# Six weight blocks converted inside the feed-forward part, and first quarters loaded and split earlier

## The chip, the cores and the metric

The kernel runs on one core of one Trainium2 chip. The metric is the device time of one execution in microseconds, lower is better. Engines are named as in the profile: PE is TensorE (PEld its weight loads), DVE is VectorE, ACT is ScalarE, POOL is GpSimd, SP is SyncE, which here only issues DMAs.

## The reference

A long convolution filters the product `x * v` along the sequence (12480 tokens, 128 channels), and two feed-forward layers with 2048 hidden units each follow:

```python
u = x * v
y = irfft(rfft(u, n=2 * S) * rfft(h_filt, n=2 * S))[:S]
x = x * y
h = x @ moe_w_in;   g = h * clip(h + 3, 0, 6) / 6;                  x = g @ moe_w_out
h = x @ moe2_w_in;  g = where(h > 0, h, exp(minimum(h, 0)) - 1);    out = g @ moe2_w_out
```

The four weight matrices arrive as float64 words (as int64) and have to become pairs of single-precision numbers, an upper and a lower part.

## The kernel before

**Two parts.** Lines up to 794 compute the convolution as four steps of dense Fourier products. The fourth step (`fourth`, products of L677 into `y`, in the order of `PARTS`) closes 17 groups; after each, `leave_y` multiplies `y` into `xp` on DVE (L754, L757). From line 795 the feed-forward part runs: 25 tiles of up to 512 tokens, for each tile 8 units of layer 1 (m = 1) and 8 of layer 2 (m = 2, 13 units behind). A unit is six products into `h` (`mm1`, L878; `h<-xs` in layer 1, `h<-x` in layer 2), an activation on ACT (`act1`, L888 for layer 1, L890 for layer 2, with a clip on POOL, L891), a gate on DVE (`gate`, L899 and L901), the upper part of the result on ACT (`hi`, L907), the lower part on DVE (`lo`, L912) and six products into `o` (`mm2`, L922). A product of 128x128 by 128x512 is issued every 0.227 us, so that 12 of them, one unit's worth, take 2.72 us.

**What sets the order.** The program is a manual schedule: each engine runs its instructions in the order in which the code wrote them, and waits where an instruction needs another engine's result. In the feed-forward loop, step n runs the list `stages`: a unit's products at step n, its `mm2` 4 (layer 1) or 5 (layer 2) steps later. `h` has three buffers, so a unit's `mm1` waits for the gate of an earlier unit; `mm2` waits for `lo`.

**Weight conversion.** `JOBS` lists 32 blocks of 256 columns (4 matrices times 8). `weight_steps` converts one block per step: a load from `in_mw` (256 KB, on SP, L262), two ACT operations (L277, L278), three DVE operations (L289, L291, L292; called a *word* below), an addition on POOL (L295) and a store of 128 KB to `w_scratch` in DRAM (L272). `convert` spreads the steps over the convolution; ten of them fall into the fourth step (`steps`).

**Weight quarters.** The feed-forward part holds each matrix in four quarters `W[i, q]` of 512 columns. `load_w` brings one back from `w_scratch` (256 KB, L737), `rounded` makes the upper part on ACT (L740), and POOL subtracts for the lower part, in one piece (`split_w`, L745) or two halves (`lower_halves`, L825). The first three, `early`, have memory of their own. The others take over the memory of the convolution's buffers; the first four of them are requested ahead of the loop. The table `pieces` gives, for each quarter, the steps n of its two halves; its upper part is made a step earlier, its load asked for five steps earlier. `lower_halves` makes POOL wait for the last gate or `lo` written before it ("pace").

**Inputs.** `split` (L838, L840) turns a tile of `xp` into its upper part (ACT) and lower part (DVE); tile 1's runs ahead of the loop.

Of the kernel before, what the change touches and what calls it, by code (L numbers as in the profile page):

```python
# [135 lines left out]
def tile_kernel(ctx, tc, xc, vc, xT, posT, w1_d, w2_d, moe_w, t1_d, gm_d, cs_d, ti_d, rows_d, column_d, ratio_d, outT):  # L136
# [17 lines left out]
    def cut(buf, size, n):  # L154
        return [buf[:, i * size:(i + 1) * size] for i in range(n)]
# [143 lines left out]
            yield  # L299
        store(len(jobs) - 1)  # L300

    weights = weight_steps(JOBS, cut(cv, 2 * WC, 3), cut(cv[:, 6 * WC:], WC, 2), cut(cv[:, 8 * WC:], WC, 4))
    RATE = 0.75
    due = [0.0]

# [309 lines left out]
    def table(i):  # L615
        return lambda: load_ti(i)
# [102 lines left out]
    def new_y(i):  # L719
# [8 lines left out]
    x0 = xs[0]  # L728

    pieces = {  # L730
        (1, 0): (1, 1), (0, 3): (1, 2), (1, 1): (3, 4), (1, 2): (5, 6), (1, 3): (7, 8), (2, 0): (9, 10), (2, 1): (11, 12),
        (3, 0): (13, 15), (2, 2): (17, 18), (3, 1): (19, 20), (2, 3): (21, 22), (3, 2): (23, 24), (3, 3): (26, 28),
    }
    next_w = list(pieces)[:4]

# [3 lines left out]
    def rounded(w):  # L739
        nc.scalar.copy(w[:, 0], w[:, 1].bitcast(F32))  # L740

    def split_w(i, q, engine=nc.gpsimd):
        w = W[i, q]
        rounded(w)
        engine.tensor_tensor(  # L745
            out=w[:, 1], in0=w[:, 1].bitcast(F32), in1=w[:, 0].bitcast(F32), op=ALU.subtract
        )

    def leave_y(i, y, widths):
        o = START.get((BATCHES[i][0][0], 1), 0)  # L750
        if len(set(widths)) == 1:
            n, w = len(widths), widths[0]
            z = xp[:, o:o + n * w].rearrange("p (b n) -> p b n", n=w)
            nc.vector.tensor_tensor(out=z, in0=y[:, :n, :w], in1=z, op=ALU.mult)  # L754
        else:
            for b, w in enumerate(widths):
                nc.vector.tensor_tensor(out=xp[:, o:o + w], in0=y[:, b, :w], in1=xp[:, o:o + w], op=ALU.mult)  # L757
                o += w
        if i == 2:
            nc.scalar.copy(x0[:, 0], xp[:, :TT])  # L760
        if i in (12, 14, 15):
            split_w(*early[(12, 14, 15).index(i)])
# [8 lines left out]
    xc6, xc7 = map(part, xs_c[6:])  # L771
    weight = [lambda p=p: load_w(*p) for p in early]
    bunches = {
        ("r", 1): [xc6, table(7)], ("m", 1): [table(8), table(9)], ("r", 6): [table(10), table(11), table(12), xc7],
        ("m", 6): [table(13)], ("r", 9): [table(14), table(15)], ("m", 10): [table(16), weight[0]], ("r", 13): weight[1:],
        ("m", 14): [],
    }
    steps = (1, 2, 4, 6, 7, 8, 10, 11, 12, 13)
    begun = {}
    for kind, i in [(kind, i) for kind, a, b in PARTS for i in range(a, b)]:  # L780
        done = i in begun
# [19 lines left out]
    for k, ((i, q), ns) in enumerate(pieces.items()):  # L801
        W[i, q] = wp.tile([128, 2, WQ], F32R, name=f"w{i}_{q}")
        if k < 4:
            load_w(i, q)
        if k > 1:
            rounds.setdefault(ns[0] - 1, []).append((i, q))
        if k > 0:
            for h, n in enumerate(ns):
                halves.setdefault(n, []).append((i, q, h))
        if k > 3:  # L810
            loads.setdefault(ns[0] - 5, []).append((i, q))

    split_w(*next_w[0])
    rounded(W[next_w[1]])

    def round_at(n):
        for p in rounds.get(n, []):
            rounded(W[p])
        for p in loads.get(n, []):
            behind(load_w(*p), paced[0])  # L820

    def lower_halves(n):
        for i, q, h in halves.get(n, []):
            w = W[i, q][:, :, h * WQ // 2:(h + 1) * WQ // 2]
            lower = nc.gpsimd.tensor_tensor(  # L825
                out=w[:, 1], in0=w[:, 1].bitcast(F32), in1=w[:, 0].bitcast(F32), op=ALU.subtract
            )
            tc.add_manual_dep(
                lower.ins, last_dve[0].ins.name,
                mybir.DependencyInfo(mybir.DependencyClass.Sync, mybir.DependencyReason.DATA), reason="pace",  # L830
            )
# [99 lines left out]
                later.setdefault(k, []).append(lambda: leave(k, m, t))  # L931


    split(-1, 1, 1, xp[:, TILES[1]])
    later.pop(0)[0]()
    stages = (
        (act1, 2, 1), (mm1, 1, 0), (lo, 2, 4), (act1, 1, 0), (gate, 1, 0), (mm2, 1, LAG - 1), (hi, 2, 3),
        (hi, 1, 1), (gate, 2, 2), (mm1, 2, 0), (lo, 1, 1), (mm2, 2, LAG),
    )
    xin[1, 0] = x0  # L940
    assert not set(halves) - set(range(1, 14)) - set(range(15, len(units)))
    for n in range(len(units) + LAG + 2):
        for f in later.pop(n, []):
            done = f()
            if done:
                last_dve[0] = done[0]
        if NU < n < len(units) and units[n][0] == 1 and units[n][2] == 2:
            load_x(n, units[n][1] + 1)
        for f, m, delay in stages:
            if 0 <= n - delay < len(units) and units[n - delay][0] == m:  # L950
                if f is gate:
                    lower_halves(n)
                f(n - delay)
            if n == 1 and f is act1 and m == 1:
                round_at(n)
        if n != 1:
            round_at(n)


# [46 lines left out]
```

## Time and profile before

| | |
|---|---|
| median of 3 runs | 1319.63 us (1319.28 to 1320.71) |
| profiled execution | 1321.85 us, its span 1320.1 us |
| PE busy | 1310.8 us of the span (99%) |
| DVE, ACT, POOL busy | 1133.2, 1006.2, 412.0 us |
| mean granted clock | 0.999 of 2.4 GHz |

The profiled execution is 2.2 us above the median, and lies 1.75 us around its span. The fourth step runs from about 215 to 252 us of the span, the feed-forward part from 251.63 us to the end. Busy shares are means over stages; which engine waits for which is read stage by stage.

### The profile page before, as it was taken

Reading aid. Unit: us, or ns where it says so; the run is one execution under the profiler, and the core shown is the slowest. Engines: PE = TensorE matmul, PEld = TensorE weight load, DVE = VectorE, ACT = ScalarE, POOL = GpSimd, SP = SyncE. Lnnn points to the kernel's source line nnn. Section 1 sums busy time; section 2 is a strip of 40 time slices with the busy share of each in tenths; the row PEclk is TensorE's granted clock in tenths of the full one; section 3 lists DMA queues with packets and bytes.
Section 4 is the critical chain, followed back from the end, with each engine's and each line's share of the span. In section 5 each row is a group of like instructions: output and inputs, shape, how many; then the busy total and the mean of one; then the engine's idle time right before and its main releaser. Section 6 shows DMA issues by size and latency. Waiting matters only on the chain.

```text
span 1320.1 us, 23000 instructions
## 1 busy us (share of the span) xinstructions
PE 1310.8 (99%) x9184; PEld 1126.8 (85%) x9184; DVE 1133.2 (86%) x1210; ACT 1006.2 (76%) x1210; POOL 412.0 (31%) x317
## 2 busy tenths in 40 slices
PE   9999999999999999999999999999999999999998
PEld 8999999888888888888888888888888888888898
DVE  6769976889988888888888888888888888898897
ACT  5677663598877888788878887888788878887876
POOL 1027741334222232323232222222222223322223
PEclk9999999999999999999999999999999999999999
DMA  8834447610000000000000000000000000000000
GB/s 276 262 124 148 133 138 234 186 48 17 9 9 0 9 8 8 9 1 9 9 9 0 9 9 8 0 9 8 8 1 9 8 9 1 8 8 9 8 3 18
DMA packets 33676, 58.80 MB, mean 45 GB/s; under 512 B 3962, under 2 KB 10272, under 8 KB 33568
## 3 DMA queue, kind: packets, MB, share of 16 engines
q1 hardware_dynamic: 28816, 53.07, 13.1%
q10 hardware_dynamic: 4752, 4.26, 0.9%
q8 instruction: 72, 1.18, 0.4%
q14 instruction: 36, 0.29, 0.1%
HBM read 46.73 MB, written 10.58 MB: 43 GB/s over the span
## 4 chain that ended last, share of the span: by engine, by line
PE 93%; DMA 2%; DVE 1%; issue 1%; ACT 1%; POOL 1%; SPq 0%; ACTq 0%; POOLq 0%; DVEq 0%
PE o L922 40%; PE h L878 39%; PE pa L401 4%; PE q L501 2%; PE z L473 2%; PE y L677 2%; PE r L454 1%; PE h L463 1%; PE q L539 1%; DMA uv<-in_vc 1%; DMA qb<-in_posT 1%; DMA w<-w_scratch 0%; POOL a L891 0%; DVE qb L487 0%; DVE au L487 0%
## 5 line engine op out<-in xcount | busy, mean ns | idle before, releaser
L922 PE MATMUL o<-gs,w 128*128 128x512 f32 (+1 forms) x2400 | 565.5, 384 | 0.0
L922 PEld LDWEIGHTS o<-gs,w 128*128 128x128 f32 x2400 | 445.2, 188 | 85.1
L891 POOL TENSOR_SCALAR a<-a 128x1024 f32<-128x1024 f32 (+1 forms) x200 | 296.6, 1483 | 707.1 <-ACT a L890 706.8
L912 DVE TENSOR_TENSOR gs<-g,gs 128x1024 fp32r<-128x1024 f32 (+1 forms) x400 | 481.1, 1203 | 5.2 <-ACT gs L907 4.4
L907 ACT CAST gs<-g 128x1024 fp32r<-128x1024 f32 (+1 forms) x400 | 409.9, 1025 | 53.1 <-DVE g L899 51.6
L899 DVE SCALAR_TENSOR_TENSOR g<-a,h 128x1024 f32<-128x1024 f32 (+1 forms) x200 | 238.7, 1194 | 116.5 <-ACT a L888 116.3
L878 PE MATMUL h<-xs,w 128*128 128x512 f32 (+1 forms) x1200 | 298.0, 384 | 1.1 <-DVE g L899 1.1
L878 PE MATMUL h<-x,w 128*128 128x512 f32 (+1 forms) x1200 | 298.0, 384 | 0.2 <-ACT a L890 0.2
L890 ACT ACTIVATE a<-h 128x1024 f32<-128x1024 f32 (+1 forms) x200 | 201.5, 1007 | 89.4 <-PE h L878 87.8
L878 PEld LDWEIGHTS h<-xs,w 128*128 128x128 f32 x1200 | 223.2, 188 | 45.8 <-DVE g L899 1.7
L878 PEld LDWEIGHTS h<-x,w 128*128 128x128 f32 x1200 | 223.1, 188 | 43.8 <-issue 0.5
L888 ACT ACTIVATE a<-h,bounds 128x1024 f32<-128x1024 f32 (+1 forms) x200 | 218.9, 1095 | 49.1 <-PE h L878 48.6
L901 DVE SCALAR_TENSOR_TENSOR g<-a,h 128x1024 f32<-128x1024 f32 (+1 forms) x200 | 237.4, 1187 | 0.2 <-POOL a L891 0.2
L295 POOL TENSOR_TENSOR cv<-cv 128x256 int32<-128x256 int32 x32 | 23.4, 732 | 121.0 <-DVE cv L292 114.7
L401 PE MATMUL pa<-tab,qb 98*64 98x180 f32 x512 | 42.7, 316 | 0.0
L401 PEld LDWEIGHTS pa<-tab,qb 98*64 98x64 f32 x512 | 39.0, 138 | 2.1
L825 POOL TENSOR_TENSOR w<-w 128x256 fp32r<-128x256 f32 x24 | 17.8, 742 | 36.3 <-DVE gs L912 17.3
L277 ACT ACTIVATE cv<-cv 128x256 int32<-128x256 uint32 x32 | 14.3, 447 | 18.7 <-DMA cv<-in_mw 10.6
L677 PE MATMUL y<-ub,qb 52*64 52x97 f32 (+3 forms) x832 | 28.2, 247 | 0.1
L677 PEld LDWEIGHTS y<-ub,qb 52*64 52x64 f32 (+1 forms) x832 | 27.0, 137 | 1.1 <-DVE au L754 0.3
L854 ACT COPY y<-o 128x512 f32<-128x512 f32 (+1 forms) x25 | 14.5, 578 | 16.7 <-PE o L922 16.7
L492 POOL TENSOR_TENSOR au<-qb,au 128x1024 f32<-128x1024 f32 (+1 forms) x12 | 26.9, 2244 | 0.5 <-DVE au L487 0.5
(101 smaller groups left out, 874.4 us busy)
## 6 DMA issues: line engine op xcount, KB each, us to landing
cv<-in_mw SPq DMA_DIRECT2D x32, 256.0 KB
uv<-in_xc SPq DMA_DIRECT2D x32, 196.0 KB
out_T<-y SPq DMA_DIRECT2D x23, 256.0 KB
qb<-in_gm SPq DMA_DIRECT2D x22, 256.0 KB
au<-in_xT SPq DMA_DIRECT2D x16, 268.0 KB
w_scratch<-cv ACTq DMA_DIRECT2D x32, 128.0 KB
w<-w_scratch SPq DMA_DIRECT2D x16, 256.0 KB
cv<-in_vc SPq DMA_DIRECT2D x20, 196.0 KB
```

The costliest lines, as they stand in the source:

```text
L401: nc.tensor.matmul(pa[f * HN:(f + 1) * HN, j, :2 * NK], lhsT=src(j, f), rhs=table[:, f], start=True, stop=True)
L492: nc.gpsimd.tensor_tensor(out=spectrum(hf, k0 + a, n), in0=m1, in1=m2[:, :, :, ::-1], op=ALU.add)
L677: anchor[0] = nc.tensor.matmul(y[c * HD:(c + 1) * HD, b, off:off + w], lhsT=lhsT, rhs=rhs[:, H1 - w:], start=(b, c) in fresh, stop=done, s ...
L878: nc.tensor.matmul(h[:, j], lhsT=wslice(2 * m - 2, a, 2 * u + j), rhs=x[:, b], start=i == 0, stop=i == 2)
L888: paced[0] = nc.scalar.activation(a, h, AF.Relu, bias=three)
L890: nc.scalar.activation(a, h, AF.Exp)
L891: nc.gpsimd.tensor_scalar(a, a, 1.0, 0.0, op0=ALU.min, op1=ALU.max)
L899: last_dve[0] = nc.vector.scalar_tensor_tensor(g, a, 6.0, h, op0=ALU.min, op1=ALU.mult)
L901: last_dve[0] = nc.vector.scalar_tensor_tensor(g, a, -1.0, h, op0=ALU.add, op1=ALU.max)
L907: nc.scalar.copy(t[:, 0], g)
L912: last_dve[0] = nc.vector.tensor_tensor(out=t[:, 1], in0=g, in1=t[:, 0].bitcast(F32), op=ALU.subtract)
L922: nc.tensor.matmul(o[:, :WID[t]], lhsT=wslice(2 * m - 1, a, 2 * u + j), rhs=gs[:, b, j], start=u == 0 and i == 0, stop=u == NU - 1 and i + ...
```

## The change

- `weight_steps` gets the first 26 blocks (`FRONT`); the fourth step holds four conversion steps (after groups 2, 6, 9, 11) and no longer ten.
- The last six blocks, quarters 1 to 3 of matrix 3, are converted in the feed-forward loop, at steps 6, 10, 15, 21, 25 and 29 (`tail`, `block_parts`). For block n: two ACT operations at the end of step n-2 (`low`), the word on DVE at the end of step n-1, POOL's addition at the start of step n's gate (`total`), the upper part on ACT at the end of step n, the lower part on POOL a step later. They use one raw buffer and two sums, and go to the weight tile without the way over DRAM. Three quarters thus lose their load, their upper part of 512 columns and their two POOL halves.
- The early quarters are requested after groups r1, m6 and m10 and split after groups 5, 9 and 13 (before: m10 and r13; 12, 14, 15).
- Ahead of the loop, three quarters are split in one piece, with no pace (before: one split, one rounded). The table `pieces` gets other steps for the rest.
- The split of tile 1's input moves from ahead of the loop to step 4.

```diff
+    FRONT = 26
+    weights = weight_steps(JOBS[:FRONT], cut(cv, 2 * WC, 3), cut(cv[:, 6 * WC:], WC, 2), cut(cv[:, 8 * WC:], WC, 4))
...
     pieces = {
-        (1, 0): (1, 1), (0, 3): (1, 2), (1, 1): (3, 4), (1, 2): (5, 6), (1, 3): (7, 8), (2, 0): (9, 10), (2, 1): (11, 12),
-        (3, 0): (13, 15), (2, 2): (17, 18), (3, 1): (19, 20), (2, 3): (21, 22), (3, 2): (23, 24), (3, 3): (26, 28),
+        (1, 0): (), (0, 3): (), (1, 1): (), (1, 2): (2, 3), (1, 3): (4, 5), (2, 0): (8, 9), (2, 1): (12, 13),
+        (3, 0): (17, 18), (2, 2): (19, 20), (2, 3): (22, 23),
     }
...
-        if i in (12, 14, 15):
-            split_w(*early[(12, 14, 15).index(i)])
+        if i in (5, 9, 13):
+            split_w(*early[(5, 9, 13).index(i)])
...
     bunches = {
-        ("r", 1): [xc6, table(7)], ("m", 1): [table(8), table(9)], ("r", 6): [table(10), table(11), table(12), xc7],
-        ("m", 6): [table(13)], ("r", 9): [table(14), table(15)], ("m", 10): [table(16), weight[0]], ("r", 13): weight[1:],
-        ("m", 14): [],
+        ("r", 1): [xc6, table(7), weight[0]], ("m", 1): [table(8), table(9)],
+        ("r", 6): [table(10), table(11), table(12), xc7], ("m", 6): [table(13), weight[1]], ("r", 9): [table(14), table(15)],
+        ("m", 10): [table(16), weight[2]], ("r", 13): [], ("m", 14): [],
     }
-    steps = (1, 2, 4, 6, 7, 8, 10, 11, 12, 13)
+    steps = (2, 6, 9, 11)
...
-    split_w(*next_w[0])
-    rounded(W[next_w[1]])
+    for p in next_w[:3]:
+        split_w(*p)
+
+    tail = dict(zip((6, 10, 15, 21, 25, 29), JOBS[FRONT:]))
...
+    def load_block(k, after=None):
+        if k < len(tail):
+            i, c = [*tail.values()][k]
+            dma = nc.sync.dma_start(raw.bitcast(I64), moe_w[i][:, c:c + WC])
+            if after is not None:
+                behind(dma, after)
...
+        def low():
+            nc.scalar.mul(s.bitcast(I32), e.bitcast(U32), 2.0 ** -29)
+            nc.scalar.activation(e, hi_word, AF.Abs)
+
+        def word():
+            v = nc.vector
+            v.tensor_scalar(e, e, MOST, LEAST, op0=ALU.min, op1=ALU.max)
+            x = e.bitcast(I32)
+            v.tensor_scalar(x, x, 3, 0x3FFFFFFF, op0=ALU.logical_shift_left, op1=ALU.bitwise_and)
+            z = hi_word.bitcast(I32)
+            last_dve[0] = v.scalar_tensor_tensor(z, z, -0x40000000, x, op0=ALU.bitwise_and, op1=ALU.bitwise_or)
+
+        def total():
+            x = s.bitcast(I32)
+            added = nc.gpsimd.tensor_tensor(out=x, in0=hi_word.bitcast(I32), in1=x, op=ALU.add)
+            at_gate(added)
+            load_block(k + 1, added)
+
+        def upper():
+            nc.scalar.copy(w[:, 0], s)
+
+        def lower():
+            at_gate(nc.gpsimd.tensor_tensor(out=w[:, 1], in0=s, in1=w[:, 0].bitcast(F32), op=ALU.subtract))
...
+    for n in tail:
+        low, word, total, upper, lower = block_parts(n)
+        at_end.setdefault(n - 2, []).append(low)
+        at_end.setdefault(n - 1, []).append(word)
+        at_start[n] = total
+        at_end.setdefault(n, []).append(upper)
+        at_start[24 if n == 21 else n + 1] = lower
...
-    split(-1, 1, 1, xp[:, TILES[1]])
-    later.pop(0)[0]()
...
-        if NU < n < len(units) and units[n][0] == 1 and units[n][2] == 2:
+        if n < len(units) and units[n][0] == 1 and units[n][2] == (2 if n > NU else 4):
             load_x(n, units[n][1] + 1)
...
+        for f in at_end.pop(n, []):
+            f()
```

The order of PE's products is the same before and after. ACT, from the end of the fourth step into the loop (`w_0` and `w_3` are quarters (1, 0) and (0, 3), `w_1` is (1, 1), `w_2` is (1, 2), `xs` tile 1's input), before:

```order
L740 CAST w_0_3440<-w_0_3440 128x512
L740 CAST w_3_3442<-w_3_3442 128x512
L838 CAST xs_3439<-au 128x512
L888 ACTIVATE a<-h,bounds 128x1024 x2
L907 CAST gs<-g 128x1024
```

and after:

```order
L741 CAST w_0_3392<-w_0_3392 128x512
L741 CAST w_3_3394<-w_3_3394 128x512
L741 CAST w_1_3396<-w_1_3396 128x512
L954 ACTIVATE a<-h,bounds 128x1024 x2
L741 CAST w_2_3398<-w_2_3398 128x512
L973 CAST gs<-g 128x1024
```

The first activation of the loop stood behind two casts of quarters and one of the input; now it stands behind three casts of quarters, and a fourth one stands ahead of the first `hi`.

DVE at steps 12 to 15, around the first gate of layer 2, before:

```order
L840 TENSOR_TENSOR x_3697<-y_3695,x_3697 128x512
L899 SCALAR_TENSOR_TENSOR g<-a,h 128x1024
L912 TENSOR_TENSOR gs<-g,gs 128x1024
L899 SCALAR_TENSOR_TENSOR g<-a,h 128x1024
L912 TENSOR_TENSOR gs<-g,gs 128x1024 x2
L899 SCALAR_TENSOR_TENSOR g<-a,h 128x1024
L901 SCALAR_TENSOR_TENSOR g<-a,h 128x1024
```

and after (`raw` is the raw block):

```order
L906 TENSOR_TENSOR x_3669<-y_3667,x_3669 128x512
L965 SCALAR_TENSOR_TENSOR g<-a,h 128x1024
L978 TENSOR_TENSOR gs<-g,gs 128x1024
L965 SCALAR_TENSOR_TENSOR g<-a,h 128x1024
L978 TENSOR_TENSOR gs<-g,gs 128x1024 x2
L851 TENSOR_SCALAR raw<-raw 128x256
L853 TENSOR_SCALAR raw<-raw 128x256
L855 SCALAR_TENSOR_TENSOR raw<-raw 128x256
L965 SCALAR_TENSOR_TENSOR g<-a,h 128x1024
L967 SCALAR_TENSOR_TENSOR g<-a,h 128x1024
```

The word of block 15 stands between two `lo` and the gate of a layer 1 unit. ACT at the same steps, before:

```order
L888 ACTIVATE a<-h,bounds 128x1024
L907 CAST gs<-g 128x1024 x2
L890 ACTIVATE a<-h 128x1024
L888 ACTIVATE a<-h,bounds 128x1024
L907 CAST gs<-g 128x1024
```

and after (`sum` is the block's sum):

```order
L954 ACTIVATE a<-h,bounds 128x1024
L973 CAST gs<-g 128x1024
L846 ACTIVATE sum_3419<-raw 128x256
L847 ACTIVATE raw<-raw 128x256
L973 CAST gs<-g 128x1024
L956 ACTIVATE a<-h 128x1024
L954 ACTIVATE a<-h,bounds 128x1024
L864 CAST w_2_3413<-sum_3419 128x256
L973 CAST gs<-g 128x1024
```

The block's two ACT operations came ahead of the activations of steps 13 and 14, and its upper part ahead of the next `hi`.

## Rows read from the trace of the kernel before

**Rows 1.** Busy time by stretch: PE, PEld, DVE, ACT, POOL, clock, DMA share, GB/s.

```profile
216.00:225.00 9.00, 8.13 (x271) 7.49 (x263) 4.66 (x12) 1.99 (x5) 0.73 (x1) 1.00 0.67 188
225.00:247.00 22.00, 21.97 (x632) 21.36 (x630) 16.43 (x33) 6.05 (x13) 5.50 (x8) 1.00 0.83 251
247.00:258.00 11.00, 9.90 (x152) 8.32 (x147) 8.40 (x12) 6.75 (x10) 6.88 (x7) 1.00 0.55 162
258.00:285.00 27.00, 27.00 (x121) 22.32 (x120) 25.87 (x25) 26.49 (x32) 7.69 (x11) 1.00 0.15 40
285.00:300.00 15.00, 15.00 (x68) 12.25 (x66) 12.20 (x11) 11.94 (x14) 5.57 (x7) 1.00 0.26 69
300.00:312.00 12.00, 12.00 (x54) 9.95 (x53) 11.69 (x11) 11.63 (x15) 6.99 (x7) 1.00 0.09 24
312.00:330.00 18.00, 18.00 (x81) 14.90 (x80) 17.60 (x14) 14.04 (x15) 6.85 (x8) 1.00 0.00 0
```

**Rows 2.** Chain that ended last, around 250 us: start us, us, what.

```profile
247.73 5.31 DMA w<-w_scratch
...
253.12 1.14 ACT w L740 x2
254.26 0.52 ACT xs L838
254.78 1.02 ACT a L888
```

**Rows 3.** Timeline, 205 to 262 us: first products of the loop, a word, POOL beside DVE.

```profile
229.31 0.30 DVE L291 TENSOR_SCALAR cv<-cv 128x256 int32<-128x256 int32 x1
229.71 0.43 DVE L292 SCALAR_TENSOR_TENSOR cv<-cv 128x256 int32<-128x256 int32 x1
...
246.61 1.28 POOL L745 TENSOR_TENSOR w<-w 128x512 fp32r<-128x512 f32 x1 [2.42 <-ACT w L740]
246.72 1.47 DVE L292 SCALAR_TENSOR_TENSOR cv<-cv 128x256 int32<-128x256 int32 x1
...
251.63 4.38 PE L878 MATMUL h<-xs,w 128*128 128x512 f32 x18
...
257.11 3.06 PE L878 MATMUL h<-xs,w 128*128 128x512 f32 x12 [1.10 <-DVE g L899]
```

**Rows 4.** Groups by line and form: one operation of a block on DVE, on ACT.

```profile
L289 DVE TENSOR_SCALAR cv<-cv 128x256 f32<-128x256 f32 x4 | 1.1, 287 | 0.0
L278 ACT ACTIVATE cv<-cv 128x256 f32<-128x256 f32 x32 | 14.4, 450 | 1.0
```

**Rows 5.** Waits of DVE from 258 to 330 us: total, times, longest.

```profile
DVE g L899 <- ACT a L888: 3.5, 4, 1.9
DVE gs L912 <- ACT gs L907: 1.0, 1, 1.0
```

**Rows 6.** Timeline, 258 to 300 us: where PE and DVE wait for each other.

```profile
280.00 0.69 DVE L840 TENSOR_TENSOR xs<-au,xs 128x512 fp32r<-128x512 f32 x1
...
282.83 1.23 DVE L912 TENSOR_TENSOR gs<-g,gs 128x1024 fp32r<-128x1024 f32 x1 [1.01 <-ACT gs L907]
...
284.48 2.88 PE L922 MATMUL o<-gs,w 128*128 128x512 f32 x12
...
291.33 1.22 DVE L899 SCALAR_TENSOR_TENSOR g<-a,h 128x1024 f32<-128x1024 f32 x1 [0.93 <-ACT a L888]
...
294.00 1.52 PE L878 MATMUL h<-xs,w 128*128 128x512 f32 x6
...
296.77 1.22 DVE L899 SCALAR_TENSOR_TENSOR g<-a,h 128x1024 f32<-128x1024 f32 x1 [1.87 <-ACT a L888]
...
298.08 1.62 PE L878 MATMUL h<-xs,w 128*128 128x512 f32 x6
```

**Rows 7.** Timeline, 299 to 332 us: a gate and the product behind it.

```profile
323.54 1.21 DVE L899 SCALAR_TENSOR_TENSOR g<-a,h 128x1024 f32<-128x1024 f32 x1
...
325.39 1.52 PE L878 MATMUL h<-xs,w 128*128 128x512 f32 x6
```

More of the change, by code (lines that the diff above doesn't have):

```diff
@@ L300, in weight_steps @@
         store(len(jobs) - 1)
-    weights = weight_steps(JOBS, cut(cv, 2 * WC, 3), cut(cv[:, 6 * WC:], WC, 2), cut(cv[:, 8 * WC:], WC, 4))
+    FRONT = 26
+    weights = weight_steps(JOBS[:FRONT], cut(cv, 2 * WC, 3), cut(cv[:, 6 * WC:], WC, 2), cut(cv[:, 8 * WC:], WC, 4))
     RATE = 0.75
@@ L804, in tile_kernel @@
             load_w(i, q)
-        if k > 1:
+        if ns:
             rounds.setdefault(ns[0] - 1, []).append((i, q))
-        if k > 0:
-            for h, n in enumerate(ns):
-                halves.setdefault(n, []).append((i, q, h))
+        for h, n in enumerate(ns):
+            halves.setdefault(n, []).append((i, q, h))
         if k > 3:
-            loads.setdefault(ns[0] - 5, []).append((i, q))
-    split_w(*next_w[0])
-    rounded(W[next_w[1]])
+            loads.setdefault(max(ns[0] - 5, 1), []).append((i, q))
@@ new lines, in tile_kernel @@
+    for p in next_w[:3]:
+        split_w(*p)
+    tail = dict(zip((6, 10, 15, 21, 25, 29), JOBS[FRONT:]))
+    for q in range(1, 4):
+        W[3, q] = wp.tile([128, 2, WQ], F32R, name=f"w3_{q}")
+    blocks = ctx.enter_context(tc.tile_pool(name="blocks", bufs=1, reuse_waits="tile"))
+    raw = blocks.tile([128, 2 * WC], F32, name="raw")
+    raws = raw.rearrange("p (n t) -> p n t", t=2)
+    sums = [blocks.tile([128, WC], F32, name=f"sum{i}") for i in range(2)]
+    def load_block(k, after=None):
[4 more added lines that the diff above has]
+                behind(dma, after)
@@ new lines, in tile_kernel, with at_gate, block_parts @@
+    load_block(0)
+    def at_gate(op):
+        tc.add_manual_dep(
+            op.ins, last_dve[0].ins.name,
+            mybir.DependencyInfo(mybir.DependencyClass.Sync, mybir.DependencyReason.DATA), reason="pace",
+        )
+    def block_parts(n):
+        k = [*tail].index(n)
+        i, c = tail[n]
+        s, e, hi_word = sums[k % 2], raws[:, :, 0], raws[:, :, 1]
+        w = W[i, c // WQ][:, :, c % WQ:c % WQ + WC]
+        def low():
[17 more added lines that the diff above has]
+            at_gate(nc.gpsimd.tensor_tensor(out=w[:, 1], in0=s, in1=w[:, 0].bitcast(F32), op=ALU.subtract))
+        return low, word, total, upper, lower
@@ L816, in round_at @@
+    at_end, at_start = {}, {}
+    for n in tail:
[5 more added lines that the diff above has]
+        at_start[24 if n == 21 else n + 1] = lower
     def round_at(n):
@@ L822, in lower_halves @@
     def lower_halves(n):
+        if n in at_start:
+            at_start.pop(n)()
         for i, q, h in halves.get(n, []):
@@ L940, in tile_kernel @@
     xin[1, 0] = x0
-    assert not set(halves) - set(range(1, 14)) - set(range(15, len(units)))
+    assert not (set(halves) | set(at_start)) - set(range(1, 14)) - set(range(15, len(units)))
+    assert not set(halves) & set(at_start)
     for n in range(len(units) + LAG + 2):
```

## The prediction

> **What bounds the kernel now.** I read the busy time by stretch first [rows 1]. PE is busy for all of 258 to 330 us, and its products are the same before and after. What the change can save is therefore idle PE time, and there is little of it where the change works: 0.87 us in 216 to 225, 0.03 in 225 to 247 and 1.10 in 247 to 258, 2.0 us in all. The same rows show who runs beside PE: from 258 to 285 DVE is busy 25.87 of 27 us and ACT 26.49. So I read the waits of DVE [rows 5] and the timelines [rows 3, 6, 7] for how much room is left before DVE makes PE wait. The reader is to see that the change takes work from a stretch in which DVE has room (16.43 of 22 us busy in 225 to 247) and puts it into the one in which it has least.
>
> **Term A, the start of the loop.** The 1.10 us idle ahead of 257.11 [rows 3] waits for the first gate, which waits for the first activation, and that is queued on ACT behind a landing [rows 2]: a quarter requested at 247.73 takes 5.31 us, two casts take 1.14, the input's cast 0.52, the activation starts at 254.78. The input's cast goes away; a third quarter and its cast (0.57) come. If the first of them still took 5.31 us and the others followed at the 251 GB/s of 225 to 247 [rows 1] (262 KB each, 1.04 us), the third would land at 255.1 and the activation start at 255.7, 0.9 us later than now: bound +0.9. If the landings cost nothing, the activation would wait for its six products alone: 18 of them take 4.38 us from 251.63 [rows 3], so six end at about 253.1, 1.6 us sooner than the activation now starts, and the whole 1.10 us goes: bound -1.1. Ahead of these transfers two raw blocks, two early quarters and at least two stores no longer stand in the last 10 us; that is over 1 MB, more than 4 us at 251 GB/s. I take -0.7, nearer to the second bound.
>
> **Term B, the fourth step.** Six words, twelve ACT operations, six loads and six stores leave it. PE idles 0.87 us there in 216 to 225, of which I can tie only a part to this work; from 225 to 247 it hardly idles, so a DVE or DMA queue that gets shorter helps nobody. Bounds 0 and -0.87; I take -0.2. A transfer that is asked for earlier (three early quarters) stands ahead of tables and inputs on SP, but the six raw loads left the same queue; I take nothing for that.
>
> **Term C, DVE in the loop.** A word on DVE is 0.29 [rows 4] plus 0.30 and 0.43 [rows 3], each waiting for the one before: about 1.1 us with the hand-overs. Six words are 6.6 us, and the split of tile 1, 0.69 [rows 6], which stood ahead of the loop, makes it 7.3 us of new DVE work between 258 and 330 us. DVE's idle time there is 27 - 25.87, 15 - 12.20, 12 - 11.69 and 18 - 17.60: 1.13, 2.80, 0.31 and 0.40, in all 4.64 us [rows 1]. The work does not fit even if every gap could be used.
>
> How much of it can be? Nearly all of it is waiting for ACT: 3.5 us for activations, 1.0 for an upper part [rows 5]. The largest gap, 1.87 us ahead of the gate at 296.77, is part of a ring: a layer 1 product ends, the activation follows, the gate follows, and the next layer 1 product needs that gate. At 298.08 the ring has no slack: the gate ends at 297.99 and the product starts 0.09 us later [rows 6]. What arrives late in this ring comes out late on PE, so the 1.87 us can't hide anything. That leaves 4.64 - 1.87 = 2.8 us.
>
> Lateness is first taken by slack. In 258 to 285: 2.2 us of words and 0.69 of split, less 1.13 idle, make DVE 1.8 us late. The lower part at 282.83 ends at 284.06; the second six of the products from 284.48, half of 2.72 us later at 285.84, need it: slack 1.8 [rows 6]. So PE gets through this stretch with at most some tenths lost, but its slack is gone. In 285 to 330: 4.4 us of words, less 2.80 + 0.31 + 0.40 - 1.87 = 1.6, add 2.8, in all 4.6 us late. Late in the stretch a gate ends at 324.75 and the product behind it starts at 325.39 [rows 7]: slack 0.6, which may be used up. 4.6 - 0.6 = 4.0 us of PE waiting.
>
> To this comes the way in which a word shares memory with POOL. At 246.61 a subtraction runs on POOL for 1.28 us; the last operation of a word starts at 246.72 and takes 1.47 us, not 0.43: it ends just after POOL [rows 3]. So a word that meets POOL can be held for up to 1.04 us. From 285 to 330 POOL is busy 19.4 of 45 us [rows 1]; four words that meet it with a chance of 43% and are held half of 1.04 would lose 0.9, two words at 28% another 0.3. Bounds 0 (they never meet) and 6 x 1.04 = 6.2 us. I take 1.2. The Trainium skill (GPSIMD Engine Reference, Specifications) says the same of the cause: POOL's interfaces to SBUF are shared with DVE, with contention for DVE instructions with two SBUF inputs or in a two-port mode. By that rule the lower parts, which have two inputs in SBUF, would be held by POOL's added operations too: six of half of 1.28 us [rows 3], so that the sum would rise by up to 3.8 us, to +8.1.
>
> ACT gets per block two operations of 0.45 [rows 4] and a cast of half 0.57 [rows 2], 1.2 us, and loses half of 0.57 for the upper part that `rounded` made: six blocks add 5.4 us. From 285 to 330 ACT idles 3.06 + 0.37 + 3.96 = 7.4 us [rows 1], where 3.6 of them come, so ACT is not short of time, but block 15's pair stands ahead of the activations of the ring, and its upper part waits for POOL, which waits for the word. I price that at nothing of its own: it makes late what is late on DVE anyway. Without that cover it would be at most 0.9 us for each of four blocks, 3.6. POOL gets two operations a block where it had one, and is busy a third of the time; hidden, except for the meetings above. Three loads of quarters, 3 x 262 KB, turn into six raw loads of the same size each at a DMA share of 0.15 and less: hidden.
>
> C is 4.0 + 1.2 = 5.2 us. Its lower bound: all 4.64 us of idle usable, no meetings: 7.3 - 4.64 - 0.6 = 2.1. Its upper bound: none usable, half of the meetings, 7.3 + 3.1 - 0.6 = 9.8.
>
> **Sum.** -0.7 - 0.2 + 5.2 = +4.3 us on the profiled execution of 1321.85, whose span is 1320.1 and which has 1.75 us around it: 1326.15. That execution lies 2.2 us above the median of the runs shown, 1319.63; I carry the difference over to the median: 1323.9 us, 0.33% slower. About 0.2%, 2.6 us, is what a measurement of this kernel can tell from no change.
>
> **Rivals.**
> - *The gaps take it (not slower).* If all of DVE's 4.64 us and the ACT gaps can be filled and no word meets POOL, C is 2.1, and with A and B the time is 1320.8. For it: most gaps are short waits for ACT that lateness closes by itself. Against it: the 1.87 us stand in the ring without slack. It is decided at the layer 1 product behind block 15's word: if DVE gets there less than 1.4 us late (the slack of the product at 294.00, behind a gate that ends at 292.55 [rows 6]), PE does not stop. 0.2.
> - *Only the savings count.* The new words cost nothing, PE's idle time of 2.0 us goes: 1317.7. The Trainium skill (Perfetto Trace Analysis, Optimization Strategy) advises to interleave regimes whose busiest engine differs, and by that rule moving words under PE's long stretch would pay. It would here if the stretch they go into had DVE to spare; the rows show 4.64 of 72 us. 0.06.
> - *The third quarter lands late.* A turns to +0.9, the words cost as forecast: 1325.5. For it: the 5.31 us of today; against it: the emptier queue. 0.14.
> - The forecast: 0.6.
>
> **How the numbers follow.** Slower by over 0.2% (above 1322.3): forecast and late landing, less their low edges, 0.72. Within 0.2%: most of the first rival, part of the second, and the forecast's low edge, 0.24. Faster by over 0.2% would need more than the 2.0 us that PE idles; 0.04 for what the profile doesn't show. The range from 1319.8 to 1326.8 takes in the first rival, the late landing, and the forecast with its meetings doubled; it leaves the second rival and the far end of C out.
>
> **What would show each step.** A: PE's wait ahead of the fourth unit's products (1.10 us now) falls below 0.6. B: PE's idle time up to the first `h` product shrinks by tenths. C: PE, never idle from 258 to 330 now, waits for gates of layer 1 (`h` behind L965), in pieces of 0.3 to 2 us, the first large one behind block 15's word, others near the words of blocks 21 and 25; single operations on `raw` take over 0.6 us beside POOL; from about 340 us on the two traces run in step. The forecast is wrong if DVE's idle time vanishes without PE stopping, or if the stops come from ACT or from quarters that come late.

## The result, and the profile after

The changed kernel takes 1326.9 us (median of 4 runs, 1326.54 to 1327.81), the kernel before 1320.17 (4 runs, 1319.28 to 1321.35): a ratio of 1.0052, 95% interval 1.0036 to 1.0068, 6.7 us slower. The forecast was 1323.9 with a range up to 1326.8. The sign and the place were right, the size was not. The profiled executions take 1326.99 (span 1325.2) and 1321.85 (span 1320.1).

Busy time by stretch of the changed kernel, in the stretches of [rows 1] from 258 us on and one more (us; PE, PEld, DVE, ACT, POOL, each with its instructions, then granted clock, DMA share, GB/s):

```profile
258.00:285.00 27.00, 26.74 (x118) 21.63 (x117) 25.44 (x28) 24.31 (x33) 7.38 (x10) 1.00 0.14 40
285.00:300.00 15.00, 12.76 (x54) 9.57 (x53) 13.64 (x15) 12.46 (x16) 5.87 (x7) 1.00 0.20 58
300.00:312.00 12.00, 11.88 (x52) 9.46 (x53) 11.77 (x12) 10.57 (x15) 6.68 (x6) 1.00 0.08 19
312.00:330.00 18.00, 16.70 (x73) 13.14 (x72) 17.30 (x18) 15.04 (x20) 6.90 (x8) 1.00 0.09 28
330.00:374.00 44.00, 43.53 (x192) 35.54 (x191) 43.93 (x38) 33.77 (x38) 10.49 (x10) 1.00 0.02 7
```

PE, never idle from 258 to 330 us before, now stops in each of these stretches. ACT idles 2.69 us from 258 to 285, where it idled 0.51, and from 330 to 374 DVE is busy 43.93 of 44 us; in the kernel before the same view has 40.12 there. Waits of PE from 245 us to the end (us in total, times, longest):

```profile
PE h L944 <- DVE g L965: 4.0, 5, 1.8
PE o L988 <- ACT gs L973: 0.3, 1, 0.3
PE h L944 <- ACT a L956: 0.2, 1, 0.2
```

Waits add up to two thirds of what is lost, since short stops and stretched products are not listed. So I compare the starts of the same products in two timelines, at three marks: the first layer 1 product (`h`), the first layer 2 product (`o`), and the `h` 64 groups of six products behind that (at 347.15 us in the kernel before). Before: 251.63, 260.00, 347.15. After: 250.94, 258.01, 352.07. So PE enters the loop 0.69 us sooner, has no stop at the start (7.07 us between the first marks, not 8.37), and then takes 94.06 us where it took 87.15. **6.91 us are lost there**, and 0.13 behind it; from 390 us to the end each activation starts 4.76 to 5.06 us later than the same one in the kernel before. Busy times in these two stretches of 64 groups, before and after, show the same from DVE's side: it is busy 8.63 us more and idle 1.72 us less (5.64 before, 3.92 after).

```profile
260.00:347.15 87.15, 87.15 (x386) 72.00 (x385) 81.51 (x71) 75.84 (x85) 31.21 (x34) 1.00 0.11 31
258.01:352.07 94.06, 89.67 (x386) 71.38 (x384) 90.14 (x89) 78.76 (x99) 32.48 (x37) 1.00 0.11 31
```

Where they are lost, as the lateness of the same product against before: -1.99 up to 281.13; -0.93 at 291.71 (1.06 lost behind block 10); +1.82 at 302.73 (2.75 behind block 15); +2.73 at 318.60 (0.91, block 21); +4.15 at 326.82 (1.42, block 25); +4.92 at 338.47 (0.77, block 29). The rows at these places, of all engines, with rows between them left out (`...`):

```profile
250.94 7.23 PE L944 MATMUL h<-xs,w 128*128 128x512 f32 x30
258.01 1.52 PE L988 MATMUL o<-gs,w 128*128 128x512 f32 x6
...
280.05 0.75 POOL L859 TENSOR_TENSOR sum<-raw,sum 128x256 int32<-128x256 int32 x1 [3.12 <-ACT gs L973]
...
280.83 0.41 ACT L864 CAST w<-sum 128x256 fp32r<-128x256 f32 x1 [0.96 <-POOL sum L859]
...
281.15 1.11 ACT L954 ACTIVATE a<-h,bounds 128x1024 f32<-128x1024 f32 x1
...
284.40 1.99 PE L988 MATMUL o<-gs,w 128*128 128x512 f32 x6 [0.26 <-ACT gs L973]
...
291.70 1.16 POOL L957 TENSOR_SCALAR a<-a 128x1024 f32<-128x1024 f32 x1 [2.40 <-ACT a L956]
...
291.87 1.13 DVE L851 TENSOR_SCALAR raw<-raw 128x256 f32<-128x256 f32 x1
...
293.78 1.21 DVE L965 SCALAR_TENSOR_TENSOR g<-a,h 128x1024 f32<-128x1024 f32 x1
...
295.05 1.67 PE L944 MATMUL h<-xs,w 128*128 128x512 f32 x6 [1.82 <-DVE g L965]
...
306.93 1.21 DVE L978 TENSOR_TENSOR gs<-g,gs 128x1024 fp32r<-128x1024 f32 x1
307.00 2.05 POOL L957 TENSOR_SCALAR a<-a 128x1024 f32<-128x1024 f32 x1 [0.30 <-ACT a L956]
...
322.68 1.21 DVE L965 SCALAR_TENSOR_TENSOR g<-a,h 128x1024 f32<-128x1024 f32 x1
322.85 0.73 POOL L859 TENSOR_TENSOR sum<-raw,sum 128x256 int32<-128x256 int32 x1 [2.16 <-DVE raw L855]
...
323.95 1.66 PE L944 MATMUL h<-xs,w 128*128 128x512 f32 x6 [1.10 <-DVE g L965]
...
325.99 1.04 POOL L957 TENSOR_SCALAR a<-a 128x1024 f32<-128x1024 f32 x1
326.08 2.02 DVE L978 TENSOR_TENSOR gs<-g,gs 128x1024 fp32r<-128x1024 f32 x1
```

Three things are to be seen. Behind block 10 ACT sits 0.96 us ahead of the upper part, whose sum comes from POOL, which waits for the word on DVE (it ends at 279.92; the row names the cast on ACT that ended 0.05 us before it); the activation whose products end at 279.9 starts at 281.15, and what follows on ACT, up to the cast at 283.31, makes PE stop at 284.40. Behind block 15 the word's first instruction takes 1.13 us beside POOL's clamp (0.29 in [rows 4], 0.28 at 321.69 here, without it), its gate starts at 293.78, and PE stops 1.82 us. And at 326.08 it isn't a word that is held but a lower part of the loop, 2.02 us where the one at 306.93 took 1.21. The two differ in who came first: at 326 the clamp started 0.09 us ahead and took 1.04, at 307 the lower part did and the clamp took 2.05.

### The profile page after: what moved, and what is told of

The parts are those of the page before. It is cut to its first block, busy times and chain, and to the rows that moved or that the text cites. A ratio compares the mean times of both kernels' runs of the same rounds, so it can differ in the third digit from the quotient of the medians.

```text
span 1325.2 us, 22940 instructions
## 1 busy us (share of the span) xinstructions
PE 1313.0 (99%) x9184; PEld 1126.2 (85%) x9184; DVE 1140.6 (86%) x1210; ACT 1003.5 (76%) x1213; POOL 406.2 (31%) x315
## 3 DMA queue, kind: packets, MB, share of 16 engines
q8 instruction: 72, 1.18, 0.4%
## 4 chain that ended last, share of the span: by engine, by line
PE 90%; DVE 3%; ACT 2%; issue 2%; POOL 1%; DMA 1%; SPq 0%; ACTq 0%; POOLq 0%; DVEq 0%
PE h L944 37%; PE o L988 37%; PE pa L402 4%; PE z L474 3%; PE y L678 3%; PE q L502 2%; PE r L455 1%; PE h L464 1%; DVE gs L978 1%; PE q L540 1%; DMA uv<-in_vc 1%; ACT a L954 1%; DVE g L965 1%; ACT gs L973 1%; POOL a L957 0%
## 5 line engine op out<-in xcount | busy, mean ns | idle before, releaser
L957 POOL TENSOR_SCALAR a<-a 128x1024 f32<-128x1024 f32 (+1 forms) x200 | 291.3, 1456 | 710.3 <-ACT a L956 710.1
L978 DVE TENSOR_TENSOR gs<-g,gs 128x1024 fp32r<-128x1024 f32 (+1 forms) x400 | 487.0, 1218 | 4.9 <-ACT gs L973 4.1
L295 POOL TENSOR_TENSOR cv<-cv 128x256 int32<-128x256 int32 x26 | 19.0, 732 | 118.5 <-DVE cv L292 99.8
L741 ACT CAST w<-w 128x512 fp32r<-128x512 f32 x13 | 8.0, 618 | 24.9 <-DMA w<-w_scratch 17.6
L755 DVE TENSOR_TENSOR au<-y,au 128x780 f32<-128x780 f32 x15 | 14.5, 969 | 13.2 <-PE y L678 12.8
```

The lines of the kernel that those rows point to most:

```text
L957: nc.gpsimd.tensor_scalar(a, a, 1.0, 0.0, op0=ALU.min, op1=ALU.max)
L978: last_dve[0] = nc.vector.tensor_tensor(out=t[:, 1], in0=g, in1=t[:, 0].bitcast(F32), op=ALU.subtract)
```

## The experiments

In all, 13 runs, three of them one of the two kernels again, in four batches, each batch with the kernel before on the same chip (1320.38, 1320.16, 1319.59 and 1319.74 us). "64 groups" is the distance from the first `o` to the `h` 64 groups behind, the stretch in which 6.91 us are lost; "start" is first `h` to first `o`; "fourth" is the first product of the fourth step to the first `h`. The last three columns come from one profiled execution each.

| kernel | us, median | ratio, 95% | fourth | start | 64 groups |
|---|---|---|---|---|---|
| before (profiled above) | 1320.17 | | 36.24 | 8.37 | 87.15 |
| before_again | 1321.93, one run | | 35.41 | 8.64 | 87.15 |
| before_timed | 1319.70 | 0.9990 to 1.0008 | 35.46 | 7.80 | 87.15 |
| after (profiled above) | 1326.90 | 1.0036 to 1.0068 | 36.26 | 7.07 | 94.06 |
| after_again | 1325.57 | 1.0029 to 1.0060 | 35.34 | 7.08 | 94.24 |
| no_words | 1320.39 | 0.9991 to 1.0009 | 35.53 | 7.05 | 87.97 |
| act_free | 1327.61 | 1.0040 to 1.0071 | 35.35 | 7.08 | 94.74 |
| pool_casts | 1324.73 | 1.0019 to 1.0044 | 34.86 | 7.07 | 92.88 |
| no_clip | 1322.42 | 1.0006 to 1.0024 | 35.13 | 7.08 | 90.92 |
| no_clip_casts | 1319.68 | 0.9993 to 1.0011 | 34.86 | 7.70 | 88.55 |
| two_blocks | 1322.26 | 1.0008 to 1.0026 | 36.95 | 7.43 | 88.64 |
| start_only | 1321.72 | 1.0002 to 1.0020 | 36.47 | 8.34 | 87.15 |
| start_early | 1321.24 | 0.9999 to 1.0017 | 36.93 | 7.64 | 87.14 |
| start_earlier | 1322.11 | 1.0011 to 1.0029 | 39.25 | 7.77 | 87.14 |
| tile_later | 1318.94 | 0.9983 to 1.0001 | 35.37 | 7.05 | 87.14 |

The last column is the one to trust: all seven executions without a word or a block in the loop have 87.14 or 87.15. What lies ahead of the loop scatters between executions of the same code: the seven kernels from after to no_clip_casts have the same program up to the loop, and their "fourth" goes from 34.86 to 36.26, their "start" from 7.05 to 7.08, but 7.70 in one.

**no_words.** The words' three DVE instructions are left out.

```diff
-        at_end.setdefault(n - 1, []).append(word)
```

> The changed kernel without the three VectorE instructions of each word (18 in all), so the weights of the last six blocks are wrong; ScalarE's and GpSimd's part of each block stays. Theory V (VectorE's added work makes all of the loss of 7.05 us between 250 and 345 us): 6 x 1.1 us and the two meetings with GpSimd (0.84 each) go, at most 0.5 us of the loss is left, 1320.0 to 1320.5 us. Theory S (ScalarE late with activations makes about half of it: its pair of 0.9 us stands ahead of the layer 1 activation): 3 us of the loss are left, 1322.5 to 1323.5 us, and PE still waits over 1 us behind block 15.

6.09 of the 6.91 us go, and the time falls to that of the kernel before. One wait of PE for a gate is left:

```profile
PE h L943 <- DVE g L964: 0.3, 1, 0.3
```

The loss needs the words on DVE. It does not follow that it is made of DVE time alone: without them ACT's waits for the sum halve as well, from 8.2 to 4.2 us between 258 and 330.

**act_free and pool_casts.** ACT's three instructions of each block, or only the upper part, go to POOL; in act_free max(x, 0) stands in for the absolute value.

```diff
-            nc.scalar.mul(s.bitcast(I32), e.bitcast(U32), 2.0 ** -29)
-            nc.scalar.activation(e, hi_word, AF.Abs)
+            nc.gpsimd.tensor_scalar(s.bitcast(I32), e.bitcast(U32), 2.0 ** -29, None, op0=ALU.mult)
+            nc.gpsimd.tensor_scalar(e, hi_word, 0.0, None, op0=ALU.max)
...
-            nc.scalar.copy(w[:, 0], s)
+            nc.gpsimd.tensor_copy(w[:, 0], s)
```

> The changed kernel with ScalarE's three instructions of each block (scale, absolute value, upper part) given to GpSimd; GpSimd's instruction keeps max(x, 0) in place of the absolute value, so some weights are wrong. VectorE's words stay where they were. Theory V: the words keep their price, 1326 to 1327 us, or more where GpSimd now meets VectorE oftener. Theory S: the pair and the wait for GpSimd's sum leave ScalarE's queue, 3 to 4 us of the 7.05 go, 1323 to 1324 us, and PE's wait behind block 15 falls from 1.82 to under 0.8 us.

> The changed kernel with only the upper part of each of the six blocks moved from ScalarE to GpSimd, so ScalarE no longer waits for GpSimd's sum (8.2 us of waits in five places); the pair ahead of each word stays on ScalarE. Theory V: 1326.5 to 1327. Theory S in its narrow form (the wait for the sum is what costs, as at block 10 where the activation starts 1.2 us after its products): the 1.0 us lost from 281 to 287 goes and a little behind block 15, 1325 to 1326 us.

With all three on POOL nothing is saved (94.74). This run does not price the pair on ACT, since POOL is then busier (13.95 us from 312 to 330, 6.90 in after) and holds DVE oftener. no_words bounds it: there the pair stays on ACT, without the words, and only 0.82 us are lost. The upper part alone saves 1.18 us of the 64 groups; its median lies 0.8 and 2.2 us below those of the changed kernel in two other batches. In pool_casts PE gets through the first stretch without a loss (in after 26.74 of 27), so the 1.06 us behind block 10 were ACT's wait for the sum, with the cast of 0.41 us behind it:

```profile
258.00:285.00 27.00, 27.00 (x121) 22.36 (x120) 26.59 (x30) 25.73 (x32) 9.34 (x12) 1.00 0.19 47
```

What is left is lost from 285 us on. Theory S falls in its wide form (no_words) and holds in its narrow one.

**no_clip and no_clip_casts.** POOL's clamp of the second unit's exponential is left out, in the second kernel with the upper part on POOL too.

```diff
             nc.scalar.activation(a, h, AF.Exp)
-            nc.gpsimd.tensor_scalar(a, a, 1.0, 0.0, op0=ALU.min, op1=ALU.max)
```

> The changed kernel without the clamp of the second unit's exponential on GpSimd (the values are wrong from there on). Theory L (a late VectorE meets the clamp in every pair: the lower part takes 2.02 us beside it where it takes 1.21, a pair takes VectorE 5.35 of PE's 5.44 us, and what is late stays late): the two words held 0.84 us and the waits behind blocks 25 and 29 (1.40 and 0.79 us) go, 3 to 4 of the 7.05 us, 1323 to 1324 us. Rival (each word costs its own 1.1 us, clamp or no clamp): only the two meetings go, 1325 to 1325.5 us, and PE still waits about 1 us each behind blocks 25 and 29.

> The changed kernel without the clamp on GpSimd (values wrong) and with the upper part of the six blocks on GpSimd instead of ScalarE. If the clamp's part (3.3 us) and the part of ScalarE's wait for the sum (1.2 us) are separate costs, both go: first loop product to hundredth activation takes 270.9 to 271.3 us, the time 1321 us, and what is left, about 2.5 us of the 7.05, is the words' own time behind block 15. If they are two views of one lateness: 272.2 us and 1322.4, as without the clamp alone.

Without the clamp 3.14 of the 6.91 us go; behind blocks 21 and 29 nothing is lost any more, behind 25 still 0.8 us, which theory L had gone. The lower parts, least, median and longest time of 33 in the 64 groups, in before, after and no_clip (ns):

```profile
L912 DVE TENSOR_TENSOR gs<-g,gs x33: 1210/1218/2027, 260.4 to 345.6; 128x1024 fp32r<-128x1024 f32 x33
L978 DVE TENSOR_TENSOR gs<-g,gs x33: 1210/1218/2030, 258.9 to 351.5; 128x1024 fp32r<-128x1024 f32 x33
L977 DVE TENSOR_TENSOR gs<-g,gs x33: 1218/1221/1226, 258.0 to 346.4; 128x1024 fp32r<-128x1024 f32 x33
```

Without the clamp no lower part and no word is held. DVE's timeline of no_clip, a gate of layer 1 and the next one, shows what that is worth:

```profile
319.37 1.21 DVE L964 SCALAR_TENSOR_TENSOR g<-a,h 128x1024 f32<-128x1024 f32 x1
...
323.90 1.22 DVE L964 SCALAR_TENSOR_TENSOR g<-a,h 128x1024 f32<-128x1024 f32 x1
```

A pair of units takes DVE 4.53 us, and PE needs 5.44 (four groups of 1.36), so 0.91 us of lateness are made good in each pair. In the kernel before the gates of such pairs are at 318.19 and 323.54, with a lower part of 2.02 between them: 5.35 us, and only 0.09 made good:

```profile
318.19 1.21 DVE L899 SCALAR_TENSOR_TENSOR g<-a,h 128x1024 f32<-128x1024 f32 x1
...
321.59 2.02 DVE L912 TENSOR_TENSOR gs<-g,gs 128x1024 fp32r<-128x1024 f32 x1
```

The clamp could cost time in two other ways: by delaying POOL's sums, or the gates of layer 2 that read its result. Neither is seen in the changed kernel from 258 to 345 us: no wait of DVE that the profile lists there ends with POOL, and POOL sits idle ahead of all six sums, until another engine is done:

```profile
POOL sum L859 <- DVE raw L855: 6.4, 4, 2.2
POOL sum L859 <- ACT gs L973: 3.1, 1, 3.1
POOL sum L859 <- PE h L944: 2.7, 1, 2.7
```

With both costs away 5.51 of the 6.91 us are gone, more than the 3.14 and 1.18 that each gives alone: they are separate costs, and each makes the other dearer. With both away the words cost 1.40, in a loop that has more room than the kernel before, which keeps its held lower parts. The "2.5 left" that I expected was too much.

**two_blocks.** Two blocks in the loop, behind units 6 and 10, upper parts on POOL, eight weight steps in the fourth step.

```diff
-    FRONT = 26
+    FRONT = 30
-    steps = (2, 6, 9, 11)
+    steps = (1, 2, 4, 6, 7, 8, 10, 11)
-    tail = dict(zip((6, 10, 15, 21, 25, 29), JOBS[FRONT:]))
+    tail = dict(zip((6, 10), JOBS[FRONT:]))
```

> Only the last two blocks are converted inside the loop, behind units 6 and 10, with the upper part on GpSimd; the other 30 before it, eight weight steps in the fourth step, the last behind table product 11 as in the changed kernel. Theory V (the words cost where VectorE has no room, from 285 us on, and fit before): no product of PE is late against the kernel before up to 340 us, the 1.3 us of the start last: 1318.5 to 1319.5 us. Rival (each word costs its 1.0 us wherever it stands): 1.3 gained, 2.1 lost, 1321 us, with PE waits behind gates between 276 and 300 us.

87.15 turn into 88.64, so 1.49 us are lost, with no word behind 285 us: PE waits for two gates, and both stops stand at 293 to 298 us, in the ring.

```profile
PE h L944 <- DVE g L965: 1.0, 2, 0.6
```

So the two early words are not swallowed by slack; DVE carries their lateness into the ring, where it comes out at 0.75 us a word.

**start_only, start_early, start_earlier.** The early quarters and the ungated splits, with all 32 blocks ahead of the loop; then the same with the weight steps sooner, twice.

```diff
-    FRONT = 26
+    FRONT = 32
-    steps = (2, 6, 9, 11)
+    steps = (1, 2, 4, 6, 7, 8, 10, 11, 12, 13)
```

In start_early the last line is (1, 2, 4, 5, 6, 7, 8, 9, 10, 11), in start_earlier (0, 1, 2, 4, 5, 6, 7, 8, 9, 10), with two more points at which raw blocks are asked for.

> The start of the change alone: three early quarters asked for sooner, the split of quarters and of the second input tile no longer ahead of the loop, but all 32 weight blocks converted before the loop as in the kernel before. Theory 1 (the whole loss is made by the work put into the loop): the 1.3 us gained at the start of the loop last, 1318.9 us where the kernel before takes 1320.2. Rival (the loop's first 80 us are bound by VectorE, so PE gives the gain back): 1320.2, no change, with PE waits behind gates between 280 and 330 us. In the first case PE never idles between 250 and 340 us.

> As the kernel with the start alone (all 32 blocks ahead of the loop), with its ten weight steps two table products sooner, so that the last store is asked for sooner. Theory Q (the third quarter comes late because raw blocks and stores stand ahead of it: it was asked for at 247.30 and took 5.42 us): it lands before 251.5, the 1.1 us wait ahead of the fourth unit goes: 0.5 to 1.3 us less than with the start alone. Rival (landings of these quarters take 5.4 us in any case): the wait of 1.1 us stays, no change.

> The start alone with its ten weight steps one more table product sooner, the last behind product 10. Theory Q: the third quarter, which with the steps up to product 11 was still awaited until 252.67 us, lands under 252 us, the wait ahead of the fourth unit's products, 0.4 us there, goes to nil, and first loop product to hundredth activation takes 268.6 to 268.8 us where the kernel before takes 269.9 to 270.1. Rival (the fourth step pays for it: VectorE at 20.07 of 22 us from 225 to 247 gets later, PE idles more there): what the loop gains is lost ahead of it, and the time stays at 1321.2.

With ten steps the third quarter does land late, as one rival had it. ACT in start_only, the last cast ahead of the activation, after a wait for the landing:

```profile
252.74 1.24 ACT L741 CAST w<-w 128x512 fp32r<-128x512 f32 x2 [1.40 <-DMA w<-w_scratch]
253.89 2.11 ACT L948 ACTIVATE a<-h,bounds 128x1024 f32<-128x1024 f32 x2
```

The start takes 8.34 us, as before. With sooner steps it falls to 7.64 and 7.77, but the fourth step pays: 39.25 us in start_earlier; the 36.93 of start_early lies only 0.5 us above the highest of the kernels with ten steps in their old places. PE in start_earlier has two stops in that step, 1.26 us ahead of 223.94 and 1.17 ahead of 243.60, which the profile puts down to nothing that it shows.

All three are slower than or level with before. What PE waits for in these two stops stays open.

**before_again, before_timed, after_again.** Both kernels once more, unchanged.

> The kernel before, profiled once more, to see how far one execution stands for the others. If the profiled execution of the first profile was late in the first 84 us, which no change touches (second stage reached at 165.7 us, the changed kernel's at 164.8), this one reaches it at 164.7 to 165.3 and takes 1319 to 1320.5 us, while first loop product to hundredth activation stays at 269.9 us. Rival: 1321.9 again, and the difference of the two kernels is 5.1 us, not 6.5.

> The changed kernel once more, for its spread: if the loop's part does not depend on the execution, first loop product to hundredth activation takes 275.4 to 275.8 us again, whatever the stages ahead of it take (second stage reached at 164.7 to 165.5, from there 84.6 to 86.1 to the first loop product). Rival: the loop's losses depend on where landings fall, and this distance moves by 1 us or more.

> The kernel before against itself, in the place of a changed kernel. If the comparison is even, 1320.0 to 1320.5 us and a ratio of 1.000; then the 1.1 to 1.9 us by which the kernels with a faster start stand above what their loops account for are made ahead of the loop. Rival (the kernel before is itself slower when it stands in that place, as its two profiled executions at 1321.85 and 1321.93 suggest): 1321 to 1322 us, and the ratios of all kernels here are high by about 0.001.

before_again took 1321.93 us, as its rival had it, though the median in that batch is 1320.16. Against itself the kernel before comes out at 0.9990 to 1.0008. At the start of the loop it is the wait ahead of the fourth unit's products that varies, 1.10 us in [rows 3]; 1.4 us in before_again, 0.6 in before_timed.

The changed kernel's loss in the loop is 7.09 us in its second execution (94.24), 0.18 more. In that one the granted clock fell to the lower level (1.2 GHz) for 3.41 us, 0.63 us after PE went on from its stop of 1.81 us for block 15's gate; in the first execution it stayed at 1.00 behind a stop of 1.82 us. Busy times of after_again in this stretch:

```profile
295.38:298.79 3.41, 3.41 (x10) 2.65 (x9) 2.01 (x3) 3.34 (x5) 1.74 (x3) 0.50 0.23 76
```

**tile_later.** The kernel before, with the cast and split of the second input tile moved from ahead of the loop to unit 4, as the change does.

```diff
-    split(-1, 1, 1, xp[:, TILES[1]])
-    later.pop(0)[0]()
...
-        if NU < n < len(units) and units[n][0] == 1 and units[n][2] == 2:
+        if n < len(units) and units[n][0] == 1 and units[n][2] == (2 if n > NU else 4):
```

> The kernel before with one thing of the change: the cast and the split of the second input tile move from ahead of the loop to unit 4; quarters, weight steps and blocks stay. Theory (ScalarE's 0.52 us of cast stand ahead of the first activation, and VectorE's 0.68 us of split fit between 258 and 285 us, where the kernels with a faster start lost nothing): first loop product to hundredth activation takes 0.5 us less than the 269.3 to 270.1 of the kernel before, 268.8 to 269.6, and the time is 1319.2 to 1320, not to be told from before by its time alone. Rival (the split makes VectorE late in the ring at 291 to 298 us, which has no slack): 269.9 or more, with a PE wait there.

1318.94 against 1319.74 us. The start takes 7.05 us, as in the changed kernel, and nothing is lost behind it. PE's rows at the start, 30 products without a stop:

```profile
249.48 7.22 PE L878 MATMUL h<-xs,w 128*128 128x512 f32 x30
256.53 1.52 PE L922 MATMUL o<-gs,w 128*128 128x512 f32 x6
```

It is the only kernel here with a median clearly below before (no_clip_casts, which computes other values, lies 0.06 us below); the interval of the times reaches 1.0001, so that it is faster rests on the marks of one execution, 0.75 to 1.6 us at the start.

## Why the prediction was right or wrong

**What bounds the kernel** was read rightly: PE stops for gates of layer 1, behind the words of blocks 15, 21 and 25 (and 29), and from 340 us on the two traces run in step but for 0.13 us. One stop came by another way, through ACT behind block 10, which the prediction had named as a sign against itself. The rival "only the savings count" falls: PE lost 6.91 us in the stretch that took the words in. The advice of the Trainium skill that stood beside it (Perfetto Trace Analysis, Optimization Strategy) is for regimes whose most-contended engine changes. This case does not test it: PE is the busiest engine in both stretches, 21.97 of 22 us and 27.00 of 27 [rows 1].

**Term A** was -0.7, measured -1.30 (8.37 to 7.07); against the three executions of before, with 7.80 to 8.64, it is -0.7 to -1.6. The sign is right; the mean, -1.2, lies just past the bound of -1.1. The reason is only half right. That more than 1 MB no longer stands ahead of the quarters is needed, as start_only shows, but only because the change brings a third quarter; tile_later has the whole gain from the tile's cast alone. Nor is the gain there each time: in no_clip_casts, whose program is that of the change up to the loop, the last of the three casts waited for its landing, and the start took 7.70:

```profile
250.53 0.62 ACT L741 CAST w<-w 128x512 fp32r<-128x512 f32 x1 [0.69 <-DMA w<-w_scratch]
```

**Term B** was -0.2. The mean of "fourth" is 35.7 us in three executions of before and 35.3 in seven with four weight steps: -0.4, inside the scatter. Nothing speaks against the step, and nothing shows it.

**Term C** is the step that failed. 5.2 was forecast, 7.04 measured (6.91 and 0.13), and its parts are less alike than the sum:

- "PE gets through this stretch with at most some tenths lost" (258 to 285 us): 1.06 us were lost, through ACT. And where ACT does not wait, as in two_blocks, the lateness reaches the ring and costs 1.49. The slack of 1.8 us at 284 belongs to one product; it does not pay back lateness that DVE carries on.
- ACT was priced "at nothing of its own: it makes late what is late on DVE anyway". Its upper part waits for POOL's sum, 8.2 us in five places from 258 to 330, and an activation stands behind it. Wait and cast are 1.18 us of the 6.91 (pool_casts), and 2.37 once the clamp is away (90.92 to 88.55). The bound of 3.6 that I had beside it held.
- The meetings were taken as 1.2 us, for words alone. Two words were held 0.84 us each, 1.7. The loop's own lower part meets the clamp too: a late DVE comes to the lower part just behind the clamp, takes 2.02 us for it, needs 5.35 us for a pair, and stays late until the next word. No step of mine had this; in [rows 1] it stands inside DVE's busy time. It is not new with the change: over the 64 groups six lower parts of the kernel before take more than 1.22 us, 3.5 us more in all, and PE does not stop; in the changed kernel seven do, 4.9 us more. So the change adds 1.7 and 1.4, 3.1 us of held time, for 1.2 in the sum, and no_clip, in which nothing is held, gives 3.14 back.
- The gaps were counted as 2.8 us that the new work can fill. DVE's idle time over the 64 groups fell by only 1.7; in pool_casts it fell by 3.5, to 2.14. So the upper parts on ACT, which wait for the sum, kept gaps open.
- The words' own lateness was taken as 4.0 us. With the other two costs away 1.40 is left, but then the 3.5 us held in the kernel before are away too, so no run prices the words alone.

So the miss of C was not in the words' price, 1.1 us each, which the rows bear out, but in held time (3.1 for 1.2) and in gaps that stayed open behind ACT (1.7 filled for 2.8). These two come to 3.0 us, where C was short by 1.8; about 0.5 goes back because the words' instructions are busy 6.1 us and not 6.6, and about 0.6 because at the end of the stretch DVE is a gate of 1.2 us further behind (33 gates in it, 34 before), where the sum allowed a slack of 0.6. Idle time is also a poor count of what DVE can make good: from 312 to 330 us it looks full in [rows 1] partly because three lower parts are held there, 0.6 to 0.8 us each, not because it has that much work.

The Trainium skill says of this port (SBUF — State Buffer, Who interferes with whom) that the pair is a lock: whichever starts first has it for the whole instruction, and the other is blocked. The trace agrees, both ways round: 2.02 for the lower part with the clamp first, 2.05 for the clamp with the lower part first. The rule that the prediction weighed (GPSIMD Engine Reference, Specifications) names the lower parts rightly, which have two SBUF inputs, but my 3.8 us by it were for POOL's added operations. All twelve of those that the blocks added run beside gates, none beside a lower part, and at 322.68 and 322.85 neither is longer than elsewhere (1.21 and 0.73).

**The sum's base.** Of the 3.0 us between 1323.9 and 1326.9, C explains 1.8, and A takes 0.6 back. The profiled executions differ by 5.1 us, the medians by 6.7, in the later batch by 6.0. The terms as measured, -1.2 for A with the mean of three executions, -0.4 for B and +7.0 to +7.2 for C, give 5.4 to 5.6. The other 0.4 to 1.3 us are not settled; they are no more than the stretch ahead of the loop scatters between executions (1.4 us in "fourth" alone). The profiled execution of the kernel before lay 2.2 us above the median that I had; that of the changed kernel lies 0.1 above its own. To carry that difference over to the changed kernel, without a margin for the scatter, made the range too narrow at its top, which the time missed by 0.1 us.

**The rivals.** "The gaps take it" was to be decided by how late DVE comes to the gate behind block 15's word: at 293.78 for an `h` that otherwise would have started at 293.07, the place was right and it was too late. "The third quarter lands late" is what happens in start_only, where it costs nothing against before (8.34, not the 0.9 us more that the rival had), and in one of seven executions with the start of the change (7.70).

## What to carry to other kernels

Before work goes onto an engine that is nearly full, look at how many us it makes good per period, and whether a shared resource changes hands when it is late: here 0.91 us a pair turns into 0.09, and what is added stays. A cast on a queue that carries activations must not wait for a result of another engine that itself waits for the added work; moved to the engine which makes the result it cost 1.2 us less. And take the parts of a change singly: the only gain of this one that the runs show was a cast moved away from the start, which needs nothing else.

## What the runs showed of the hardware that was not expected

Which of two engines is held at the shared port can hang on a start 0.07 or 0.09 us sooner. In the steady part of both kernels the lower parts take 1.2 us (294 of 295 between 400 and 1200 us in the kernel before) and the clamp gives way, with 1.5 to 2.2 us instead of 1.04 (143 of 147). After a disturbance the two can stay in the other order for many pairs: in no_words a lower part still takes 2.02 us at 346.68, where PE no longer stops: 5.35 us a pair are less than 5.44.

The granted clock of PE can fall inside the loop. Behind two nearly equal stops it stayed at 1.00 in one execution of the changed kernel (1.82 us) and fell to 0.50 for 3.41 us in the other (1.81 us); whether the stop brings it, and what decides it, is not shown.
